# First attention pair rearranged, and one step of the feed-forward moved into the last pair

## The chip, the cores and the metric

The kernel runs on one NeuronCore of a Trainium2 chip. TensorE (PE) multiplies matrices; VectorE (DVE), ScalarE (ACT) and GpSimd (POOL) do the elementwise work; SyncE (SP) issues the loads. The engines run side by side and meet at semaphores; each takes its own instructions in order. The metric is the device time of one execution in microseconds (us), lower is better. Before the change it is 503.4 us, the median of three runs (503.26 to 503.74).

## What is computed

Attention over 2 batches x 12 heads, 448 tokens, head size 64, all fp32, then two feed-forward blocks on the 896 tokens:

```python
scores = cap * np.tanh(q @ k.T / np.sqrt(64) / cap)     # cap = 30
attn = np.exp(scores - max) / (sum + 1e-09);  x = attn @ v
h = x @ w_in                                            # 768 -> 1024
solu = h * softmax(h)
x = ((solu - mean) / sqrt(var + 1e-06) * g_ln) @ w_out  # 1024 -> 768
g = x @ w_gate;  val = x @ w_val                        # 768 -> 1536
out = silu(g) * val @ w_out2                            # 1536 -> 768
```

The weights come as float64 and are rounded to fp32 on the chip. Each product whose operands are split into a high and a low part (`hi`, `lo`) is three matmuls (hi*hi, hi*lo, lo*hi); the sums S, the products with v (pv) and the warm products are plain fp32 and are recorded as two instructions each.

## The kernel before

Attention goes over 12 pairs of heads (`attn_pair`, L276). A pair has these steps:

- `attn_load` (L180): q, k and v of the pair, each as two loads of 112 KB on SyncE's queue.
- `attn_T` (L192): TensorE transposes q and k into a PSUM tile T, four pieces each; then the high part is copied out of T by ScalarE (by VectorE for pair 1) and the low part is subtracted by VectorE. Both go to `ks`. For pair 0 that is done for k first and then for q, in one T tile of two banks; for the other pairs k and q go together.
- `attn_qk` (L208): chunk c of four: six matmuls `sc` over the two heads, into one of two score buffers, then one tanh on ScalarE (112 x 896).
- `attn_exp` (L223): one exp on ScalarE over two chunks.
- `attn_sums`, `attn_recip`, `attn_pv`, `attn_norm` (L229 to L274) of the pair before: column sums S by TensorE, their reciprocals by GpSimd and VectorE (the tiles tr and sm), the products pv, and x = pv * tr split into hi and lo.

Between them VectorE makes a twelfth of w_in per pair out of float64 (the tiles wi). While `in_order` is set (all of attention), each engine's instructions stay in the order of the code; after L553 a scheduler may move them. Pair 0 and pair 1 take chunks 2 and 3 late in the pair (`early` is false); from pair 2 on they come right after the first exp. A thirteenth call of `attn_pair` finishes pair 11, and three of the six steps of h_0 (the first 128 tokens of x @ w_in, six matmuls a step) fill in there; the other three follow (L550 to L552). Then h_1, h_2, ... come, each with a softmax tail on VectorE and ScalarE (`tail`, L368).

PSUM has eight banks. Up to L557 two pools hold them: `psc` two score buffers of two banks, and `ptA` one buffer for each tag, laid out in the order in which the tags are first used: pv (the warm products use it too), t (two banks: T, and h_0), S. Then the pool `pm` (L560) takes all eight as buffers of one bank each; a tile of `pm` can be written only when the last reader of what lay in its bank is done. The two tail reads of h_0 that come last are these, one for each half f of h:

```python
self.V.scalar_tensor_tensor(ef, ef, sm[:, 6:7], h[f], op0=ALU.mult, op1=ALU.mult,
```

`keep_warm(n)` (L174) issues n products of zeros that nothing reads.

Of the kernel before, what the change touches and what calls it, by code (L numbers as in the profile page):

```python
# [5 lines left out]
F32 = mybir.dt.float32  # L6
# [30 lines left out]
class Kernel:  # L37
# [154 lines left out]
    def attn_T(self, i):  # L192

        CP, S = self.CP, self.S
        r = self.raws[i]
        ks = r["ks"] = self.at.tile([128, 2, 2, S], F32R, name=f"ks_{i}", tag="ks", bufs=2)
        ps = self.pt.tile([128, 2, 512], F32, name=f"T_{i}", tag="t")
        lots = ("k", "q") if i == 0 else ("kq",)
        for names in lots:
            for n in names:  # L200
                m = "kq".index(n)
                for c in range(4):
                    self.transpose(ps[:, m, c * CP:(c + 1) * CP], r[n][:, c * 128:(c + 1) * 128], self.ident[:CP, :CP])
            m = slice("kq".index(names[0]), "kq".index(names[-1]) + 1)
            (self.hi_dve if i == 1 else self.hi_act)(ks[:, m, 0], ps[:, m, :S])
            self.lo_dve(ks[:, m, 1], ps[:, m, :S], ks[:, m, 0])

    def attn_qk(self, i, c):  # L208

# [66 lines left out]
    def attn_pair(self, i, fill=()):  # L276


        last, n = i - 1, 2 * self.NP
        if i == 0:  # L280
            self.attn_load(2, "v")
            self.w_in_load(1)
        elif i + 2 < n:
            self.attn_load(i + 2)
        w = self.w_steps[i]

        early = i > 1
        w[0]()
        if i < n:
            self.attn_qk(i, 0)  # L290
            self.attn_qk(i, 1)
        if i + 1 < n:
            self.attn_T(i + 1)
        if i < n:
            self.attn_exp(i, 0)
            if early:
                self.attn_qk(i, 2)
                self.attn_qk(i, 3)
        for f in fill:
            f()  # L300
        if i:
            self.attn_sums(last)
        w[1]()
        w[2]()
        if i:
            self.attn_pv(last, 0)
            self.attn_pv(last, 1)
            self.attn_recip(last)
        w[3]()
        if i < n:  # L310
            if not early:
                self.attn_qk(i, 2)
                self.attn_qk(i, 3)
            self.attn_exp(i, 1)
        if i:
            self.attn_pv(last, 2)
            self.attn_pv(last, 3)
            self.attn_norm(last)
# [198 lines left out]
    def run(self):  # L517
# [7 lines left out]
        self.at = self.pool("at", side="right")  # L525
        psc = self.psc = self.pool("psc", bufs=2, space=PSUM)
        ptA = self.pt = self.ph = self.pool("ptA", bufs=1, space=PSUM)
        self.attn_load(0, "kq")
        self.setup()
        self.attn_load(1, "kq")  # L530
        self.wi = [self.slot(f"wi{u}", [128, KD, F1], f"wi{u}") for u in range(2)]
# [3 lines left out]
        w = [self.w_in_steps(i) for i in range(2 * KD)]  # L535
        none = lambda: None
        w = [(none,) * 4] + w + [(none,) * 4]
        self.w_steps = [(w[i][1], w[i][2], w[i + 1][0], w[i][3]) for i in range(2 * KD + 1)]
        self.attn_T(0)
        self.keep_warm(4)  # L540
        self.attn_load(0, "v")
        self.attn_load(2, "kq")
        self.w_in_load(0)
        self.attn_load(1, "v")
        nc.sync.dma_start(self.gt, self.g_ln.rearrange("(f p) -> p f", p=128))
        h = [self.ff1_h(t) for t in range(7)]
        for i in range(2 * self.NP):
            self.attn_pair(i)
        self.htag = "t"
        self.attn_pair(2 * self.NP, [f for _, f in h[0][:3]])  # L550
        for _, f in h[0][3:]:
            f()  # L552
        self.in_order = False  # L553
        self.at.release()
# [110 lines left out]
```

## Time and profile before

| | |
|---|---|
| median of 3 runs | 503.4 us |
| the profiled execution | 504.33 us |
| its span, first to last instruction | 502.0 us |
| PE busy, DVE busy, ACT busy | 492.1 (98%), 351.9 (70%), 251.1 (50%) us |
| mean granted TensorE clock | 0.997 |
| attention, about | 0 to 118 us |
| h and its tails, about | 117 to 176 us |

The profile is one execution; times in it count from the first instruction. A row of the timeline gives start and length of a group of equal instructions, and in brackets how long the engine stood idle before it and which instruction's end released it. A granted clock of 1.00 is 2.4 GHz, 0.50 is 1.2 GHz.

### The profile page before, as it was taken

The numbers are of one execution on the slowest core, as the hardware profiler recorded it, in microseconds if no ns is written. First come the engines' busy times: TensorE is split into PE (matmuls) and PEld (weight loads), VectorE is DVE, ScalarE is ACT, GpSimd is POOL, SyncE is SP. The second block draws the span as 40 slices with busy tenths as digits, with TensorE's granted clock in tenths as the row PEclk, the third lists the DMA queues.
The fourth block names the chain that finished last, engine by engine and source line by source line (L and its number), as shares of the span: only waits on it lengthen the run. The fifth ranks groups of instructions, "written<-read, shape, count | busy, mean of one in ns | idle before, by whom it ended". The sixth has DMA issues, their size and how long they took to land.

```text
span 502.0 us, 7647 instructions
## 1 busy us (share of the span) xinstructions
PE 492.1 (98%) x3016; PEld 406.1 (81%) x3016; DVE 351.9 (70%) x633; ACT 251.1 (50%) x373; POOL 21.9 (4%) x62
## 2 busy tenths in 40 slices
PE   7899999999999999999999999999999999999996
PEld 6454545456788899898899998889999989999996
DVE  2689999984778894769899999788997867200000
ACT  4999999961224695666544454444434434100000
POOL 1112121210000010000000000000000000000000
PEclk9899999999999999999999999999999999999999
DMA  6856564311000222243535445446344525111111
GB/s 146 218 130 165 129 164 117 103 44 42 1 0 23 76 73 85 85 146 128 185 127 164 151 144 172 125 127 188 96 126 104 179 64 157 33 33 31 33 31 31
DMA packets 66916, 52.40 MB, mean 104 GB/s; under 512 B 35904, under 2 KB 62272, under 8 KB 66880
## 3 DMA queue, kind: packets, MB, share of 16 engines
q1 hardware_dynamic: 66112, 51.13, 35.3%
q10 hardware_dynamic: 736, 0.79, 0.4%
q8 instruction: 23, 0.38, 0.3%
q14 instruction: 13, 0.11, 0.1%
q0 software_dynamic: 32, 0.00, 0.0%
HBM read 49.16 MB, written 2.75 MB: 103 GB/s over the span
## 4 chain that ended last, share of the span: by engine, by line
PE 94%; ACT 3%; DVE 2%; issue 0%; POOL 0%; POOLq 0%
PE o L29 17%; PE g L29 17%; PE v L29 17%; PE x L29 11%; PE h L29 10%; PE pv L29 7%; PE sc L29 6%; PE S L29 4%; PE T L29 2%; ACT P L29 2%; PE lt L29 1%; DVE sm L29 1%; PE warm L29 1%; DVE e L29 0%; ACT e L29 0%
## 5 line engine op out<-in xcount | busy, mean ns | idle before, releaser
L29 PE MATMUL g<-x,y 128*128 128x512 f32 (+1 forms) x432 | 91.2, 363 | 0.0
L29 PE MATMUL v<-x,y 128*128 128x512 f32 (+1 forms) x432 | 90.5, 362 | 0.0
L29 PEld LDWEIGHTS g<-x,y 128*128 128x128 f32 x432 | 78.5, 188 | 8.9
L29 PEld LDWEIGHTS v<-x,y 128*128 128x128 f32 x432 | 78.2, 188 | 8.5
L29 PE MATMUL h<-wi,x 128*128 128x512 f32 x252 | 58.9, 392 | 0.0
L29 PEld LDWEIGHTS h<-wi,x 128*128 128x128 f32 x252 | 46.9, 188 | 11.0 <-issue 1.5
L29 PE MATMUL o<-x,a 128*128 128x384 f32 x294 | 52.3, 334 | 0.0
L29 PEld LDWEIGHTS o<-x,a 128*128 128x128 f32 x294 | 51.1, 188 | 0.0
L29 ACT ACTIVATE P<-sc,consts 112x896 f32<-112x896 f32 x48 | 45.8, 1009 | 5.7 <-PE sc L29 5.7
L29 ACT ACTIVATE P<-P,consts 112x1792 f32<-112x1792 f32 x24 | 43.0, 1794 | 0.5
L29 PE MATMUL sc<-ks 64*112 64x448 f32 x288 | 37.0, 385 | 2.7 <-ACT P L29 2.4
L504 ACT ACTIVATE ob<-o 128x384 f32<-128x384 f32 x14 | 6.9, 492 | 64.0 <-PE o L29 64.0
L29 PE MATMUL pv<-P,v 112*32 112x448 f32 x384 | 38.5, 539 | 0.0
L29 PE MATMUL x<-lB,wo 128*128 128x256 f32 (+1 forms) x192 | 37.3, 338 | 0.4 <-ACT lB L29 0.4
L29 PEld LDWEIGHTS sc<-ks 64*112 64x112 f32 x288 | 23.3, 174 | 17.3 <-issue 6.6
L29 PE MATMUL o<-y,a 128*128 128x384 f32 x189 | 34.1, 334 | 0.0
L29 PEld LDWEIGHTS x<-lB,wo 128*128 128x128 f32 x192 | 30.1, 189 | 3.6 <-ACT lB L29 0.6
L29 PEld LDWEIGHTS o<-y,a 128*128 128x128 f32 x189 | 32.9, 188 | 0.1
L29 PEld LDWEIGHTS pv<-P,v 112*32 112x32 f32 x384 | 12.3, 110 | 23.5 <-issue 23.2
L29 PE MATMUL x<-lA,wo 128*128 128x384 f32 x144 | 28.5, 336 | 0.0
L29 PEld LDWEIGHTS x<-lA,wo 128*128 128x128 f32 x144 | 25.1, 188 | 1.1
L29 DVE SCALAR_TENSOR_TENSOR w<-w_raw,w 128x768 uint32<-128x768 uint32 (+1 forms) x26 | 23.1, 891 | 0.3
(90 smaller groups left out, 628.1 us busy)
## 6 DMA issues: line engine op xcount, KB each, us to landing
wg_raw<-in_moe_w_gate_dram SPq DMA_DIRECT2D x12, 768.0 KB, 4.2
wv_raw<-in_moe_w_val_dram SPq DMA_DIRECT2D x12, 768.0 KB, 4.2
w_raw<-in_moe_w_out_dram SPq DMA_DIRECT2D x11, 768.0 KB, 4.5
wi_raw<-in_moe_w_in_dram SPq DMA_DIRECT2D x12, 512.0 KB, 4.7
wo_raw<-in_moe_w_out_dram SPq DMA_DIRECT2D x12, 512.0 KB, 3.4
k<-in_k_dram SPq DMA_DIRECT2D x24, 112.0 KB, 2.9
q<-in_q_dram SPq DMA_DIRECT2D x24, 112.0 KB, 4.0
v<-in_v_dram SPq DMA_DIRECT2D x24, 112.0 KB, 2.9
```

The costliest lines, as they stand in the source:

```text
L29: i = f(*a, **k)
L504: nc.scalar.activation(ob, acc, AF.Copy)
```

## The change

Pair 0: q is loaded and transposed ahead of k, into a tile of its own (with the tag S, one bank), and k into a one-bank tile of tag t. k's high and low parts are made for the first chunk (112 columns) and then for the other 336. The four chunks of pair 0 are issued in a row, then pair 1's transposes, then 14 warm products. Two warm products stand after q's transposes; the four after both are gone. Pair 1 takes chunks 2 and 3 early. The first step of h_0 moves from the thirteenth call into pair 11, between its chunks 1 and 2; the other five come after pair 11's pv.

```diff
--- before.py
+++ after.py
@@ -194,16 +194,23 @@
         CP, S = self.CP, self.S
         r = self.raws[i]
         ks = r["ks"] = self.at.tile([128, 2, 2, S], F32R, name=f"ks_{i}", tag="ks", bufs=2)
-        ps = self.pt.tile([128, 2, 512], F32, name=f"T_{i}", tag="t")
-        lots = ("k", "q") if i == 0 else ("kq",)
-        for names in lots:
-            for n in names:
-                m = "kq".index(n)
+        if i:
+            ps = self.pt.tile([128, 2, 512], F32, name=f"T_{i}", tag="t")
+            lots = [(ps, "kq", S)]
+        else:
+            ps = [self.pt.tile([128, 512], F32, name=f"T_{n}", tag=t) for n, t in (("q", "S"), ("k", "t"))]
+            lots = [(p.unsqueeze(1), n, w) for p, n, w in zip(ps, "qk", (S, CP))]
+        for ps, names, w in lots:
+            for j, n in enumerate(names):
                 for c in range(4):
-                    self.transpose(ps[:, m, c * CP:(c + 1) * CP], r[n][:, c * 128:(c + 1) * 128], self.ident[:CP, :CP])
+                    self.transpose(ps[:, j, c * CP:(c + 1) * CP], r[n][:, c * 128:(c + 1) * 128], self.ident[:CP, :CP])
             m = slice("kq".index(names[0]), "kq".index(names[-1]) + 1)
-            (self.hi_dve if i == 1 else self.hi_act)(ks[:, m, 0], ps[:, m, :S])
-            self.lo_dve(ks[:, m, 1], ps[:, m, :S], ks[:, m, 0])
+            for a in (slice(0, w), slice(w, S)):
+                if a.start < a.stop:
+                    (self.hi_dve if i == 1 else self.hi_act)(ks[:, m, 0, a], ps[:, :, a])
+                    self.lo_dve(ks[:, m, 1, a], ps[:, :, a], ks[:, m, 0, a])
+            if names == "q":
+                self.keep_warm(2)
 
     def attn_qk(self, i, c):
 
@@ -284,20 +291,24 @@
             self.attn_load(i + 2)
         w = self.w_steps[i]
 
-        early = i > 1
         w[0]()
         if i < n:
             self.attn_qk(i, 0)
             self.attn_qk(i, 1)
+        if i == 0:
+            self.attn_qk(i, 2)
+            self.attn_qk(i, 3)
         if i + 1 < n:
             self.attn_T(i + 1)
+        if i == 0:
+            self.keep_warm(14)
+        for f in fill:
+            f()
         if i < n:
             self.attn_exp(i, 0)
-            if early:
-                self.attn_qk(i, 2)
-                self.attn_qk(i, 3)
-        for f in fill:
-            f()
+        if 0 < i < n:
+            self.attn_qk(i, 2)
+            self.attn_qk(i, 3)
         if i:
             self.attn_sums(last)
         w[1]()
@@ -308,9 +319,6 @@
             self.attn_recip(last)
         w[3]()
         if i < n:
-            if not early:
-                self.attn_qk(i, 2)
-                self.attn_qk(i, 3)
             self.attn_exp(i, 1)
         if i:
             self.attn_pv(last, 2)
@@ -525,7 +533,7 @@
         self.at = self.pool("at", side="right")
         psc = self.psc = self.pool("psc", bufs=2, space=PSUM)
         ptA = self.pt = self.ph = self.pool("ptA", bufs=1, space=PSUM)
-        self.attn_load(0, "kq")
+        self.attn_load(0, "qk")
         self.setup()
         self.attn_load(1, "kq")
         self.wi = [self.slot(f"wi{u}", [128, KD, F1], f"wi{u}") for u in range(2)]
@@ -537,18 +545,17 @@
         w = [(none,) * 4] + w + [(none,) * 4]
         self.w_steps = [(w[i][1], w[i][2], w[i + 1][0], w[i][3]) for i in range(2 * KD + 1)]
         self.attn_T(0)
-        self.keep_warm(4)
         self.attn_load(0, "v")
         self.attn_load(2, "kq")
         self.w_in_load(0)
         self.attn_load(1, "v")
         nc.sync.dma_start(self.gt, self.g_ln.rearrange("(f p) -> p f", p=128))
         h = [self.ff1_h(t) for t in range(7)]
+        self.htag = "t"
         for i in range(2 * self.NP):
-            self.attn_pair(i)
-        self.htag = "t"
-        self.attn_pair(2 * self.NP, [f for _, f in h[0][:3]])
-        for _, f in h[0][3:]:
+            self.attn_pair(i, [f for _, f in h[0][:1]] if i == 2 * self.NP - 1 else ())
+        self.attn_pair(2 * self.NP)
+        for _, f in h[0][1:]:
             f()
         self.in_order = False
         self.at.release()
```

TensorE's order at the start, before the change (T is the tile of the transposes, sc_0 to sc_3 the chunks; numbers behind names are buffers):

```order
L29 MATMUL warm<-z 64x64 x18
L29 MATMUL T_129<-ident,k_73 128x112 x4
L29 MATMUL T_129<-ident,q_76 128x112 x4
L29 MATMUL warm<-z 64x64 x4
L29 MATMUL sc_0_168<-ks_128 112x448 x6
L29 MATMUL sc_1_176<-ks_128 112x448 x6
L29 MATMUL T_185<-ident,k_119 128x112 x4
L29 MATMUL T_185<-ident,q_122 128x112 x4
L29 MATMUL sc_2_204<-ks_128 112x448 x6
L29 MATMUL sc_3_212<-ks_128 112x448 x6
L29 MATMUL sc_0_233<-ks_184 112x448 x6
L29 MATMUL sc_1_241<-ks_184 112x448 x6
```

The same stretch after it:

```order
L29 MATMUL warm<-z 64x64 x18
L29 MATMUL T_q<-ident,q_73 128x112 x4
L29 MATMUL warm<-z 64x64 x2
L29 MATMUL T_k<-ident,k_76 128x112 x4
L29 MATMUL sc_0_169<-ks_128 112x448 x6
L29 MATMUL sc_1_177<-ks_128 112x448 x6
L29 MATMUL sc_2_186<-ks_128 112x448 x6
L29 MATMUL sc_3_194<-ks_128 112x448 x6
L29 MATMUL T_203<-ident,k_119 128x112 x4
L29 MATMUL T_203<-ident,q_122 128x112 x4
L29 MATMUL warm<-z 64x64 x14
L29 MATMUL sc_0_249<-ks_202 112x448 x6
```

Pair 1's transposes moved behind all four chunks of pair 0, and 14 products stand between them and pair 1's first chunk.

TensorE's order at the end of attention, where h_0's last step meets h_1 (h_1_0 and h_1_1 are the two halves of h_1; in brackets which engine's semaphore the instruction waits for), before:

```order
L29 MATMUL h_0_1366<-wi0_125,x_127 128x512 [waits DVE_49]
L29 MATMUL h_0_1366<-wi1_126,x_127 128x512
L29 MATMUL h_0_1366<-wi1_126,x_127 128x512 [waits DVE_49]
L29 MATMUL h_0_1366<-wi0_125,x_127 128x512 x2
L29 MATMUL h_1_0_1479<-wi0_125,x_127 128x512
L29 MATMUL h_1_1_1480<-wi0_125,x_127 128x512 [waits PE_49]
```

and after the change:

```order
L29 MATMUL h_0_1315<-wi0_125,x_127 128x512 [waits DVE_49]
L29 MATMUL h_0_1315<-wi1_126,x_127 128x512
L29 MATMUL h_0_1315<-wi1_126,x_127 128x512 [waits DVE_49]
L29 MATMUL h_0_1315<-wi0_125,x_127 128x512 x2
L29 MATMUL h_1_0_1495<-wi0_125,x_127 128x512
L29 MATMUL h_1_1_1496<-wi0_125,x_127 128x512 [waits DVE_49]
```

The order is the same; h_1_1's first matmul waited for TensorE's own S of pair 11 and now waits for VectorE. In the built program T and h_0 lay in banks 5 and 6 and S in bank 7; now S has bank 5, and T and h_0 have 6 and 7, since pair 0's q takes the tag S ahead of the tag t. h_1_1 lies in bank 7 in both. The VectorE instruction that it waits for now is the read of h_0's second half named above.

TensorE around the last pair (pair 11's chunks, then sums and pv of pairs 10 and 11), before:

```order
L29 MATMUL sc_0_1283<-ks_1203 112x448 x6
L29 MATMUL sc_1_1291<-ks_1203 112x448 x6
L29 MATMUL sc_2_1301<-ks_1203 112x448 x6
L29 MATMUL sc_3_1309<-ks_1203 112x448 x6
L29 MATMUL S_1317<-P_0_1186,ones 32x448 x4
```

and after:

```order
L29 MATMUL sc_0_1299<-ks_1219 112x448 x6
L29 MATMUL sc_1_1307<-ks_1219 112x448 x6
L29 MATMUL h_1315<-wi_125,x 128x512 x2
L29 MATMUL h_1315<-wi_126,x 128x512 x2
L29 MATMUL h_1315<-wi_125,x 128x512 x2
L29 MATMUL sc_2_1324<-ks_1219 112x448 x6
```

Six of h_0's 36 matmuls came forward; the twelve that followed them between pv of pair 10 and S of pair 11 went behind pv of pair 11.

## Rows read from the trace of the kernel before

**Rows 1.** Chain that ended last, shares of the span by engine.

```profile
PE 94%; ACT 3%; DVE 2%; issue 0%; POOL 0%; POOLq 0%
```

**Rows 2.** Second load of q: its issue (start, length), then size and landing.

```profile
2.84 0.62 SPq L190 DMA_DIRECT2D q<-in_q_dram  x1
...
q<-in_q_dram SPq DMA_DIRECT2D x1, 112.0 KB, 3.3
```

**Rows 3.** Timeline of PE, first pairs: start, length, what, idle before it and releaser.

```profile
4.90 0.57 PE L29 MATMUL T<-ident,k 112*128 112x112 f32 x4
6.76 0.60 PE L29 MATMUL T<-ident,q 112*128 112x112 f32 x4 [1.29 <-DVE ks L29]
7.30 0.68 PE L29 MATMUL warm<-z 128*64 128x64 f32 x8
...
14.04 2.36 PE L29 MATMUL sc<-ks 64*112 64x448 f32 x12 [1.79 <-ACT P L29]
...
24.23 1.47 PE L29 MATMUL sc<-ks 64*112 64x448 f32 x12
...
33.12 1.48 PE L29 MATMUL sc<-ks 64*112 64x448 f32 x12
...
36.84 1.71 PE L29 MATMUL S<-P,ones 112*32 112x448 f32 x16
...
41.49 1.47 PE L29 MATMUL sc<-ks 64*112 64x448 f32 x12
```

**Rows 4.** Timeline of ACT, first two pairs, and the last exp of attention.

```profile
7.40 0.54 ACT L29 ACTIVATE ks<-T 128x448 fp32r<-128x448 f32 x1 [1.35 <-PE T L29]
9.36 1.91 ACT L29 ACTIVATE P<-sc,consts 112x896 f32<-112x896 f32 x2 [1.41 <-PE sc L29]
...
16.62 1.89 ACT L29 ACTIVATE P<-sc,consts 112x896 f32<-112x896 f32 x2
18.40 0.92 ACT L29 ACTIVATE ks<-T 128x896 fp32r<-128x896 f32 x1
...
22.10 1.91 ACT L29 ACTIVATE P<-sc,consts 112x896 f32<-112x896 f32 x2 [1.11 <-PE sc L29]
...
106.57 1.79 ACT L29 ACTIVATE P<-P,consts 112x1792 f32<-112x1792 f32 x1
```

**Rows 5.** Windows: busy us (count) of PE, PEld, DVE, ACT, POOL; clock, DMA share, GB/s.

```profile
14.50:15.00 0.50, 0.49 (x6) 0.07 (x4) 0.05 (x1) 0.47 (x2) 0.00 (x0) 0.74 0.96 110
15.00:15.50 0.50, 0.50 (x4) 0.43 (x6) 0.47 (x2) 0.50 (x1) 0.00 (x0) 0.50 0.55 38
...
18.00:18.50 0.50, 0.50 (x9) 0.23 (x12) 0.00 (x0) 0.50 (x2) 0.00 (x0) 0.84 0.82 279
```

**Rows 6.** Timeline of PE, end of attention and first rows of h.

```profile
100.11 1.48 PE L29 MATMUL sc<-ks 64*112 64x448 f32 x12
102.08 1.75 PE L29 MATMUL sc<-ks 64*112 64x448 f32 x12 [0.49 <-ACT P L29]
...
117.37 12.58 PE L29 MATMUL h<-wi,x 128*128 128x512 f32 x54
130.47 1.09 PE L29 MATMUL lt<-ident,e 128*128 128x128 f32 x8 [0.53 <-DVE e L29]
```

**Rows 7.** Timeline of DVE: pair 0's low part, pair 1's high part.

```profile
7.98 0.62 DVE L29 TENSOR_TENSOR ks<-T,ks 128x448 fp32r<-128x448 f32 x1 [1.27 <-ACT ks L29]
10.88 1.09 DVE L29 CAST ks<-T 128x896 fp32r<-128x896 f32 x1 [2.27 <-PE T L29]
```

**Rows 8.** Timeline of DVE: normalization of pair 10, then the tail of h_0.

```profile
105.53 0.65 DVE L29 STREAM_TRANSPOSE tr<-S 128x448 f32<-128x448 f32 x1 [1.24 <-PE S L29]
...
109.54 0.61 DVE L29 TENSOR_TENSOR x<-pv,tr 128x448 f32<-128x448 f32 x1
...
121.82 1.29 DVE L29 TENSOR_REDUCE sm<-h 128x1 f32<-128x512 f32 x2 [2.17 <-PE h L29]
...
126.72 0.73 DVE L29 SCALAR_TENSOR_TENSOR e<-e,sm,h 128x512 f32<-128x512 f32 x1
```

## The prediction

> **What bounds the kernel now.** I read the chain that ended last first: TensorE holds 94% of it, ScalarE 3% [rows 1]. So what counts is where TensorE stands still, and the timelines of TensorE and of the engines that it waits for come next. Two places matter. At the start TensorE waits for the first pair's softmax: its second transposes wait 1.29 us, and before 14.04 it is idle for 1.79 us [rows 3], while ScalarE from 9.36 to 16.62 has no gap [rows 4]. From 33.12 on a pair takes 41.49 - 33.12 = 8.37 us without a stall [rows 3]. At the end of attention it waits 0.49 us once more, and from 117.37 on 54 matmuls of h run as one stream up to the first transposes of h_0's result, which wait 0.53 us for VectorE [rows 6]. A third thing is the clock: 0.74 in the half microsecond from 14.50, 0.50 from 15.00, and 0.84 in that from 18.00 [rows 5]. By these shares it is at 1.2 GHz from about 14.74 to 18.16, right after the idle 1.79 us; 3.4 us at half rate lose 1.7 us of matmul time.
>
> **First pair.** The second load of what comes second lands at 2.84 + 3.3 = 6.1 [rows 2]; that is k now, of the same size. T_k no longer shares a tile with what is read, so its transposes run from 6.15 to 6.75 instead of from 6.76 [rows 3]; q's two parts are made in the meantime. ScalarE's copy of 448 columns takes 0.54, of 896 0.92 [rows 4], so 0.38 per 448 and 0.26 for 112; VectorE's 0.62 and 1.09 [rows 7] give 0.27. So the first chunk's high part is there at 7.05, its low part at 7.4. Twelve score matmuls, two chunks, take 1.48 us [rows 3]; one chunk issues in half of that, 0.7, and with the run-out of its last matmul, which the half doesn't shorten, I take 0.95: begun at 7.1 it ends at 8.05, and tanh starts there instead of at 9.36: 1.3 earlier. The other 336 columns: ScalarE's 0.45 wait until VectorE has read the first part, then VectorE takes 0.51, so that chunk 1 is done at 8.9, under the first tanh, which ends at 9.05: nothing.
>
> ScalarE then does the same four tanh and two exp in another order, 7.26 us as before (9.36 to 16.62, [rows 4]), plus 0.06 since chunk 2 has to wait for a score buffer: pair 1's tanh starts at 15.4, not 16.62. Behind it pair 1's chunk 3 starts when the second tanh ends, at 15.4 + 1.9 = 17.3, lasts 0.7, and S and pv (41.49 - 36.84 = 4.65, [rows 3]) bring pair 2's first chunk to 22.7; before it was at 24.23. Pair 2 then took 33.12 - 24.23 = 8.89, since ScalarE came late after its 1.11 us wait [rows 4]; that wait goes, so pair 2 takes 8.37. Pair 3 starts at 31.05 instead of 33.12: **-2.05 us**.
>
> What I cost at nothing: pair 1's transposes move behind four chunks and end at 10.05 + 0.7 + 1.0 = 11.75 (chunk 3 starts when the second tanh ends); VectorE's two copies of 1.09 [rows 7] end at 14.0, pair 1's first chunk at 14.7, under ScalarE's 15.4. The 14 warm products are 28 instructions; eight took 0.68 [rows 3], so 28 take some 1.8 and end at 13.5, before the copies. If that cover went (the products at half rate, 3.0 us), it would cost 0.15. The two products after T_q end before k has landed. SyncE's queue only swaps two loads, and a load of w_in passes half a load of k that is used a pair later. In the new order no idle stretch of TensorE is longer than 0.6 us, so I let the clock stay up. Bounds: -2.5 (if ScalarE never waits and the period is even shorter at first) and -0.4 (if the clock falls all the same and 1.7 come back).
>
> **Last pair.** Six matmuls of h_0 come between chunks 1 and 2. In the stream of 54 one takes 12.58 / 54 = 0.23 [rows 6]. The six, 1.5 us with the change of shape, fill the 0.49 and the 0.27 by which the second twelve (1.75) are longer than the first (1.48) [rows 6]: -0.75. The price: pv of pair 11 now comes right behind S of pair 11, and its bank is free only when VectorE has read pair 10's pv. That read ends 110.15 - 105.53 = 4.62 after VectorE's first transpose [rows 8]. Counted from 100.11, S of pair 10 starts after 1.4 + 1.5 + 1.4 at 104.4, so this transpose comes at 104.4 + 1.71 = 106.1 and the read ends at 110.75; TensorE is there after S, pv (4.65) and S again (1.5), at 110.55, and waits 0.2. The last exp ends at 106.57 + 1.79 = 108.36 [rows 4], before S of pair 11 at 109.05. Together **-0.5**, between 0 and -0.75.
>
> **The bank of h_1.** This part the diff does not name. h_1's second half lies in bank 7, which was S's and is now h_0's second half. TensorE takes its instructions in order, so it stops at the first matmul of that half until VectorE's second read of e<-e,sm,h ends, at 126.72 + 0.73 = 127.45 in the old times [rows 8]. Before, that matmul was number 20 of the stream of 54: 117.37 + 19 x 0.233 = 121.8 [rows 6]. The wait is 127.5 - 121.8 = 5.7 us. The tail itself doesn't move against h_0's end: VectorE was idle for 2.17 us before it [rows 8] and has nothing more to do now. The 35 matmuls left take 35 x 0.233 = 8.15, so the transposes of h_0 come at 135.65 instead of 130.47: the 0.53 us wait there is swallowed. **+5.2**, and I know no cover: nothing but h_1 is in the queue.
>
> A pause of 5.6 us is three times the 1.79 after which the clock fell [rows 5]. I take one stretch at half rate like that one, from the restart on: **+1.7**; bounds 0 (it is up again when work resumes) and 3.4 (twice as long).
>
> On the banks the Trainium skill has a rule (Perfetto Trace Analysis, section Matmuls): matmul groups that don't depend on each other should rotate through different PSUM banks, so that the evacuation of one overlaps the next group's matmuls. The trace agrees for the old layout: the stream of 54 ran straight on while VectorE read h_0 [rows 6, 8]. By that rule the overlap of 5.7 us is lost for as long as one bank is shared, and the sum is the one above.
>
> Behind that all is TensorE's stream again: h_1's tail starts when h_1 ends, as before.
>
> **Sum.** -2.05 - 0.5 + 5.2 + 1.7 = +4.35, against the profiled execution's 504.33 (span 502.0, 2.3 around it): 508.7 there. That execution is 0.9 above the median of 503.4, so I set the change on the median: 507.7.
>
> **Rivals.**
> 1. The clock does not cost: it is up when work resumes. For it: in the first pair it fell only 0.7 us after the matmuls had begun again. Against it: the pause is three times as long. Sum +2.65, 506.0. The skill (TensorE: Matmul & The Clock Gate, section Why this matters for your kernels) says that an idle gap between bursts takes the engine back to half rate, which speaks against this rival; no run here shows a gap of this length.
> 2. The clock stays low twice as long: +6.05, 509.4.
> 3. The first pair gains next to nothing, as k lands late or the clock falls there still: -0.4 in place of -2.05, +6.0, 509.4. Against it: landing is read from a row, and ScalarE's chain starts 1.3 earlier by terms of which none is above 0.6.
> 4. The other side: h_1_1 doesn't hold TensorE up, because other matmuls pass the one that waits. Then -2.05 - 0.5 remain: 500.8, faster. It decides as soon as the engine can find 5.6 us of work behind it; the 35 matmuls of h_1 include 17 that write the other half. Against it: while the transposes of h_0 waited 0.53 us, no matmul of h_2 ran, though nothing held these back but their place [rows 6]. If half of the wait went so, the sum would be about nothing: 503.4.
>
> **Chances.** Forecast (507.7, with 506.8 to 508.7) 0.64; rival 1 0.13; rival 2 0.08; rival 3 0.06; rival 4 0.06 with all its gain and 0.03 with half. Below 505.3 lie rival 4's 0.09; above 509.2 about half of rivals 2 and 3, 0.07: the range is 505.3 to 509.2. About 0.2%, 1 us, is what a measurement can tell from no change. Faster 0.06, same 0.03, slower 0.91.
>
> **What would show it.** The first tanh at about 8.05, pair 3's first chunk at 31, no clock below 1.00 before 100; h's six matmuls between the last pair's chunks with no wait there; then an idle time of about 5.6 us on TensorE at h, released by VectorE's e, and a clock of 0.50 around the restart; the transposes of h_0 without a wait. I am wrong if the stream of h has no such gap, if the clock is 1.00 right behind it, or if pair 3 starts after 32.

## The result and the profile after

The changed kernel takes 508.02 us, the median of five runs (507.82 to 508.87), against 503.4 before: 1.0092 of it, with a 95% interval of 1.0079 to 1.0106. It is slower by 4.6 us, where 507.7 was forecast.

The profiled execution has a span of 506.2 us, 4.2 more than before. The rows below come from it, in the order of the prediction. First TensorE's timeline from the start to pair 3 (start and length in us, what, idle before it and who ended that), against [rows 3]:

```profile
5.02 0.98 PE L29 MATMUL T_q<-ident,q 112*128 112x112 f32 x4
...
6.31 0.60 PE L29 MATMUL T_k<-ident,k 112*128 112x112 f32 x4
7.27 1.79 PE L29 MATMUL sc<-ks 64*112 64x448 f32 x12 [0.35 <-ACT ks L29]
...
11.88 1.84 PE L29 MATMUL warm<-z 128*64 128x64 f32 x28
...
22.73 1.48 PE L29 MATMUL sc<-ks 64*112 64x448 f32 x12
...
31.12 1.48 PE L29 MATMUL sc<-ks 64*112 64x448 f32 x12
```

The waits of 1.29 and 1.79 us are gone; the longest left in this stretch is 0.35. Pair 2 begins at 22.73 instead of 24.23, pair 3 at 31.12 instead of 33.12. ScalarE, against [rows 4]:

```profile
6.95 0.26 ACT L29 ACTIVATE ks<-T_k 128x112 fp32r<-128x112 f32 x1 [0.37 <-PE T_k L29]
...
8.18 3.90 ACT L29 ACTIVATE P<-sc,consts 112x896 f32<-112x896 f32 x4 [0.17 <-PE sc L29]
...
15.34 1.89 ACT L29 ACTIVATE P<-sc,consts 112x896 f32<-112x896 f32 x2
...
23.64 1.01 ACT L29 ACTIVATE P<-sc,consts 112x896 f32<-112x896 f32 x1 [0.31 <-PE sc L29]
```

The four tanh of pair 0 stand in one row from 8.18 on (9.36 before), and the wait of 1.11 us ahead of pair 2's tanh is 0.31. So the first pair does what the change says. TensorE from pair 11 on, against [rows 6]:

```profile
98.16 1.47 PE L29 MATMUL sc<-ks 64*112 64x448 f32 x12
99.56 1.66 PE L29 MATMUL h<-wi,x 128*128 128x512 f32 x6
101.15 1.49 PE L29 MATMUL sc<-ks 64*112 64x448 f32 x12
...
107.10 1.69 PE L29 MATMUL S<-P,ones 112*32 112x448 f32 x16
109.06 3.21 PE L29 MATMUL pv<-P,v 112*32 112x448 f32 x32 [0.27 <-DVE x L29]
112.20 7.36 PE L29 MATMUL h<-wi,x 128*128 128x512 f32 x31
125.05 9.93 PE L29 MATMUL h<-wi,x 128*128 128x512 f32 x35 [5.49 <-DVE e L29]
134.82 1.04 PE L29 MATMUL lt<-ident,e 128*128 128x128 f32 x8
```

Here most of the loss sits in a single row. Before, 54 matmuls of h ran as one stream; now the stream breaks after 31, TensorE stands 5.49 us, and `<-DVE e` names VectorE's read of h_0. Pair 11 was 1.95 us early at 98.16, and h_0's transposes (lt) are 4.35 us late at 134.82. VectorE's tail of h_0, against [rows 8], shows which read ends the wait:

```profile
124.27 0.73 DVE L29 SCALAR_TENSOR_TENSOR e<-e,sm,h 128x512 f32<-128x512 f32 x1
...
127.16 0.81 DVE L29 TENSOR_SCALAR e<-e,sm 128x1024 f32<-128x1024 f32 x1
```

The second `e<-e,sm,h` ends at 125.00, and TensorE goes on at 125.05. The tail of h_0 ends at 127.97 while TensorE is still busy, so lt, which waited 0.53 us for it before, waits no more. The clock around the pause, in windows of half a microsecond (columns as in [rows 5], the clock third from the end):

```profile
121.50:122.00 0.50, 0.00 (x0) 0.00 (x0) 0.00 (x0) 0.50 (x3) 0.00 (x0) 0.89 0.00 0
122.00:122.50 0.50, 0.00 (x0) 0.00 (x0) 0.07 (x1) 0.40 (x2) 0.00 (x0) 0.50 0.00 0
...
128.50:129.00 0.50, 0.50 (x3) 0.36 (x3) 0.00 (x0) 0.00 (x0) 0.00 (x0) 0.78 0.00 0
129.00:129.50 0.50, 0.50 (x4) 0.41 (x3) 0.00 (x0) 0.00 (x0) 0.00 (x0) 1.00 0.00 0
```

The granted clock goes to 1.2 GHz during the pause and stays there until about 128.7, some 3.7 us behind the restart. Over the first 100 us the column reads 1.00, through the stretch too in which it was 0.50 before. (In the first 6 us it disagrees with the durations: q's four transposes at 5.02 took 0.98 us and k's four at 6.31 took 0.60, both at a granted clock of 1.00.)

### The profile page after: what moved, and what is told of

Read it like the earlier page. It is cut to its first block, busy times and chain, and to the rows that moved or that the text cites. A ratio compares the mean times of both kernels' runs of the same rounds, so it can differ in the third digit from the quotient of the medians.

```text
span 506.2 us, 7696 instructions
## 1 busy us (share of the span) xinstructions
PE 494.4 (98%) x3040; PEld 408.6 (81%) x3040; DVE 352.1 (70%) x634; ACT 250.9 (50%) x374; POOL 21.3 (4%) x62
## 4 chain that ended last, share of the span: by engine, by line
PE 96%; DVE 2%; ACT 1%; issue 0%; POOL 0%; POOLq 0%
PE o L29 17%; PE g L29 17%; PE v L29 17%; PE h L29 12%; PE x L29 11%; PE pv L29 7%; PE sc L29 6%; PE S L29 4%; PE T L29 2%; PE lt L29 1%; PE warm L29 1%; DVE sm L29 1%; DVE ks L29 0%; ACT P L29 0%; ACT e L29 0%
## 5 line engine op out<-in xcount | busy, mean ns | idle before, releaser
L29 PE MATMUL h<-wi,x 128*128 128x512 f32 x252 | 60.8, 400 | 5.5 <-DVE e L29 5.5
L29 PEld LDWEIGHTS h<-wi,x 128*128 128x128 f32 x252 | 48.0, 193 | 16.9 <-DVE e L29 5.9
```

What stands on the lines that cost most here:

```text
L29: i = f(*a, **k)
```

## The experiments

The theory is the prediction's: the bank of h_1 costs about 5 us of waiting and 1.7 us of clock, and the two parts that the change is about gain some 2.5. The rival is that the loss comes from the new order of the instructions itself. All times are medians, and each ratio is against the kernel before, run on the same chip. The runs on h's step alone, on k in one piece, on the products left out and on before's places for the chunks shared a second chip, on which before takes 503.63 us against 503.43 on the first, so between the two groups 0.2 us of difference means nothing.

**The banks put back.** In the changed kernel k's tile is allocated ahead of q's. That changes no instruction and no place in any engine's row, but T and h_0 lie in banks 5 and 6 again and S in 7.

```
-            ps = [self.pt.tile([128, 512], F32, name=f"T_{n}", tag=t) for n, t in (("q", "S"), ("k", "t"))]
-            lots = [(p.unsqueeze(1), n, w) for p, n, w in zip(ps, "qk", (S, CP))]
+            pk, pq = [self.pt.tile([128, 512], F32, name=f"T_{n}", tag=t) for n, t in (("k", "t"), ("q", "S"))]
+            lots = [(p.unsqueeze(1), n, w) for p, n, w in zip((pq, pk), "qk", (S, CP))]
```

> The changed kernel with T_k's tile taken ahead of T_q's, so that T and h_0 lie in banks 5 and 6 and S in 7 again; every engine's order is that of the changed kernel. Bank theory: the pause in h (5.49 us) and the half-rate stretch behind it go, the first pair's 2.0 us and the last pair's 0.6 us stay: 500.8 us (500.3 to 501.3), the stream of h through the tail of h_0 has no gap, and the transposes of h_0 wait about 0.5 us for VectorE again. Rival (the move of h_0's steps does it: all of h_0 now stands right ahead of h_1, with nothing between): as slow as the changed kernel, 508.

Measured: 501.32 us, ratio 0.9959 (0.9947 to 0.9972). TensorE's timeline at the end of attention in this kernel:

```profile
98.20 1.47 PE L29 MATMUL sc<-ks 64*112 64x448 f32 x12
...
109.09 3.21 PE L29 MATMUL pv<-P,v 112*32 112x448 f32 x32 [0.26 <-DVE x L29]
112.24 15.26 PE L29 MATMUL h<-wi,x 128*128 128x512 f32 x66
128.02 1.09 PE L29 MATMUL lt<-ident,e 128*128 128x128 f32 x8 [0.53 <-DVE e L29]
```

The 66 matmuls run as one stream, and lt waits 0.53 us as it did before the change. h's stream begins within 0.04 us of the changed kernel's, and lt then comes 6.80 us earlier. So the layout of the banks alone costs 508.02 - 501.32 = 6.7 us, and the rest of the change gains: the rival is out.

**The banks alone, in the kernel before.** One of its 18 first warm products gets a tile of tag S ahead of T; nothing else is touched.

```
-        self.keep_warm(18)
+        self.keep_warm(17)
+        self.keep_warm(1, "S")
...
-    def keep_warm(self, n):
-        ps = self.pt.tile([128, 512], F32, name="warm", tag="pv")
+    def keep_warm(self, n, tag="pv"):
+        ps = self.pt.tile([128, 512], F32, name="warm", tag=tag)
```

> The kernel before with one of its 18 first warm products put into a tile of the tag S, ahead of T: S gets bank 5 there, T and h_0 get 6 and 7; every engine's order is that of before. Bank theory: the wait alone, 5.7 us less the 0.53 us swallowed at the transposes, and 1.6 us of half rate behind it: 510.2 us (509.3 to 510.9). Rival (the move of h_0's steps does it): 503.4.

Measured: 510.39 us, ratio 1.0140 (1.0126 to 1.0154), so 7.0 us more. The same row appears on TensorE:

```profile
116.89 4.64 PE L29 MATMUL h<-wi,x 128*128 128x512 f32 x19
127.02 10.10 PE L29 MATMUL h<-wi,x 128*128 128x512 f32 x35 [5.49 <-DVE e L29]
```

The stream breaks after 19 matmuls, the number that the prediction counted in the old order, for the same 5.49 us. Counted from pair 11's first chunk (99.58) to lt (136.95), so without what the first pair did in this execution, it is 37.37 us against 130.47 - 100.11 = 30.36 before [rows 6]: 7.0 again. The price goes with the banks in either order of instructions.

**The pause filled.** In the changed kernel 44 products of zeros stand between h_0 and h_1; the wait stays.

```
+        self.keep_warm(44)
```

> The changed kernel with 44 warm products (88 instructions, 0.058 us each, 5.1 us) between h_0's last step and h_1. If the clock is a term of its own: it stays at 1.00, the 35 matmuls of h_1 behind the wait take 8.1 us instead of 9.93, and the time falls by 1.7 to 506.3 (505.9 to 506.8) though the wait stays where it is. Rival (the pause is all the cost, the clock costs nothing): 508.0, or a little more if the products end late.

Measured: 506.54 us, ratio 1.0058 (1.0046 to 1.0071).

```profile
112.54 7.10 PE L29 MATMUL h<-wi,x 128*128 128x512 f32 x30
119.57 5.35 PE L29 MATMUL warm<-z 128*64 128x64 f32 x88
124.84 8.72 PE L29 MATMUL h<-wi,x 128*128 128x512 f32 x36
133.40 1.04 PE L29 MATMUL lt<-ident,e 128*128 128x128 f32 x8
```

The clock is 1.00 behind the products, too:

```profile
125.00:125.50 0.50, 0.49 (x2) 0.18 (x3) 0.47 (x2) 0.00 (x0) 0.00 (x0) 1.00 0.00 0
```

From the start of h's stream to lt it takes 133.40 - 112.54 = 20.86 us; in the changed kernel it was 134.82 - 112.20 = 22.62, with the banks put back 128.02 - 112.24 = 15.78. The products end at 119.57 + 5.35 = 124.92, and VectorE's read that frees the bank at 125.30 in this execution, so they don't lengthen the wait. By the traces, then, the wait costs 20.86 - 15.78 = 5.1 us and the low clock 22.62 - 20.86 = 1.8; by the medians the clock costs 508.02 - 506.54 = 1.5. Part of that difference arises ahead of h: pair 11 began 0.35 us later in the profiled execution of this kernel (98.51 against 98.16).

**The move of h's step alone.** In the kernel before, the first step of h_0 goes between chunks 1 and 2 of pair 11 and the rest behind pv(11). Its first pair and its banks stay.

```
-            if early:
-                self.attn_qk(i, 2)
-                self.attn_qk(i, 3)
         for f in fill:
             f()
+        if i < n and early:
+            self.attn_qk(i, 2)
+            self.attn_qk(i, 3)
...
+        self.htag = "t"
         for i in range(2 * self.NP):
-            self.attn_pair(i)
-        self.htag = "t"
-        self.attn_pair(2 * self.NP, [f for _, f in h[0][:3]])
-        for _, f in h[0][3:]:
+            self.attn_pair(i, [f for _, f in h[0][:1]] if i == 2 * self.NP - 1 else ())
+        self.attn_pair(2 * self.NP)
+        for _, f in h[0][1:]:
```

> The kernel before with h_0's first step moved into pair 11 as in the change, and the other five behind pv of pair 11; nothing else, banks as before. By the sum: the 0.49 and 0.27 us at pair 11's chunks go, 0.27 come at pv of pair 11: 502.9 (502.6 to 503.2). Rival (h_0's steps one after the other cost more than that): 503.4 or above.

Measured: 503.04 us over eleven runs, ratio 0.9986 (0.9975 to 0.9998); before on the same chip 503.63, so 0.6 us less. The interval reaches from 0.1 to 1.3 us, so the size rests on TensorE's rows:

```profile
99.71 1.48 PE L29 MATMUL sc<-ks 64*112 64x448 f32 x12
101.12 1.66 PE L29 MATMUL h<-wi,x 128*128 128x512 f32 x6
...
110.59 3.21 PE L29 MATMUL pv<-P,v 112*32 112x448 f32 x32 [0.24 <-DVE x L29]
...
129.51 1.09 PE L29 MATMUL lt<-ident,e 128*128 128x128 f32 x8 [0.53 <-DVE e L29]
```

From pair 11's first chunk to lt it takes 29.80 us, against 130.47 - 100.11 = 30.36 before [rows 6]: 0.56 less, with the new wait at pv that the prediction named.

**k in one piece.** With the banks put back, k's parts are made for all 448 columns at once.

```
-            lots = [(p.unsqueeze(1), n, w) for p, n, w in zip((pq, pk), "qk", (S, CP))]
+            lots = [(p.unsqueeze(1), n, w) for p, n, w in zip((pq, pk), "qk", (S, S))]
```

> As e1_banks_back, but k's high and low parts are made for all 448 columns at once. If the split in 112 and 336 columns counts: the first chunk's low part is ready some 0.5 us later (0.54 and 0.62 us instead of 0.26 and 0.27), the first tanh starts at 8.75 instead of 8.18, and as ScalarE is the chain from there to pair 2, the time is 0.5 above e1_banks_back, 501.8. Rival (one extra wait in the split eats it: the 336 columns wait for VectorE): the same as e1_banks_back, 501.3.

Measured: 501.63 us, ratio 0.9964 (0.9951 to 0.9976); 0.3 above the version with k split, of which 0.2 can be the chip. The timeline of ScalarE shows the first tanh at 8.63, behind a longer wait:

```profile
8.63 3.88 ACT L29 ACTIVATE P<-sc,consts 112x896 f32<-112x896 f32 x4 [1.22 <-PE sc L29]
```

With k split it starts at 8.21 in the kernel with the banks put back, and pair 3 at 31.16 instead of 31.53. But k's load landed later there: its transposes began at 6.38, and here at 6.26. Counted from them, the first tanh comes 2.37 us later without the split and 1.83 with it, and pair 3 is 0.49 later. By the traces, one execution each, the split of k is worth about 0.5 us of the first pair's gain, as expected; the medians alone don't show it.

**The warm products left out.** With the banks put back, the 14 products ahead of pair 1's first chunk go.

```
-        if i == 0:
-            self.keep_warm(14)
```

> As e1_banks_back without the 14 warm products behind pair 1's transposes. TensorE then stands still for about 1.9 of the 2.3 us from 11.95 to 14.25. If the products hold the clock: it falls to 0.50 for some 3.4 us, pair 1's transposes for pair 2 and its chunks run at half rate, 0.5 to 1.5 us lost, 502.2. Rival (ScalarE is the chain there and hides it, or the clock holds): 501.3.

Measured: 501.47 us, ratio 0.9965 (0.9953 to 0.9977). The five executions lie apart: 502.31 and 502.29, with a mean clock of 0.996, and 501.21 to 501.47, with 0.998 to 1.000. The profiled one is of the first kind:

```profile
13.06 0.46 PE L29 MATMUL sc<-ks 64*112 64x448 f32 x2 [1.28 <-DVE ks L29]
14.10 1.61 PE L29 MATMUL sc<-ks 64*112 64x448 f32 x10 [0.57 <-DVE ks L29]
...
23.79 1.47 PE L29 MATMUL sc<-ks 64*112 64x448 f32 x12
```

Its clock in windows:

```profile
14.50:15.00 0.50, 0.50 (x8) 0.45 (x6) 0.00 (x0) 0.50 (x1) 0.00 (x0) 0.83 1.21 182
15.00:15.50 0.50, 0.50 (x4) 0.06 (x2) 0.00 (x0) 0.50 (x2) 0.00 (x0) 0.50 0.63 31
...
18.00:18.50 0.50, 0.50 (x8) 0.40 (x6) 0.47 (x2) 0.50 (x2) 0.00 (x0) 0.75 0.78 194
```

TensorE waits 1.28 and 0.57 us, the clock falls just behind, and pair 2 comes at 23.79 instead of 22.77. So both theories hold, each in some executions: without the products the clock falls in some of them and that costs 1.0 us, and in the others the products are worth nothing. The median hides this. Only the fall in the profiled execution is seen in a trace; the other four are told apart by their mean clock and time alone. The edit also lets two loads of w_in change places with half a load of k on SyncE's queue, but behind pair 0 TensorE waits for no load in this trace.

**Before's places for chunks 2 and 3.** With the banks put back, pairs 0 and 1 issue these chunks where the kernel before had them, and the 14 products go.

```
-        if i == 0:
-            self.attn_qk(i, 2)
-            self.attn_qk(i, 3)
...
-        if i == 0:
-            self.keep_warm(14)
...
-        if 0 < i < n:
+        if 1 < i < n:
...
+            if i < 2:
+                self.attn_qk(i, 2)
+                self.attn_qk(i, 3)
```

> As e1_banks_back, but pairs 0 and 1 take chunks 2 and 3 where the kernel before has them, and the 14 warm products are left out. If the new place of the chunks gives the second part of the 2.0 us: the first tanh is early as in e1_banks_back (8.18, against 9.36), but TensorE pauses again ahead of pair 1, the clock falls there, and pair 2 starts 1.2 and not 1.5 us early and has its 0.5 us stall: 502.1 (501.8 to 502.4). Rival (the gain is all from q and k at the start): 501.3.

Measured: 503.4 us over twelve runs, but from 501.58 to 505.73; ratio 0.9992 (0.9978 to 1.0006). Neither number was met. The profiled execution, one of 503.95 us, shows why the time doesn't answer the question. On TensorE, up to pair 3:

```profile
12.71 1.77 PE L29 MATMUL sc<-ks 64*112 64x448 f32 x12 [1.49 <-ACT P L29]
...
21.52 1.47 PE L29 MATMUL sc<-ks 64*112 64x448 f32 x12
...
25.76 1.01 PE L29 MATMUL T<-ident,q 112*128 112x112 f32 x4 [2.23 <-DMA q<-in_q_dram]
26.70 2.55 PE L29 MATMUL sc<-ks 64*112 64x448 f32 x12
```

and on SyncE's queue:

```profile
18.15 0.57 SPq L190 DMA_DIRECT2D q<-in_q_dram  x1
18.82 0.56 SPq L89 DMA_DIRECT2D wi_raw<-in_moe_w_in_dram  x1
19.43 0.56 SPq L190 DMA_DIRECT2D q<-in_q_dram  x1
```

In the kernel with the banks put back the two half loads of q stood together here, at 17.97; the edit has put a load of w_in between them. In this execution q's transposes waited 2.23 us for their load, and the next twelve score matmuls took 2.55 us, as the clock was 0.50 from 26.00 to 29.00. The fastest runs, 501.58 and 501.64, are 0.3 above the kernel with the banks put back, 0.2 of which can be the chip. That the load was in time in those is a guess, so what the row of four chunks is worth over the whole kernel stays open.

Ahead of that wait, though, the trace speaks against the theory. TensorE stood for 1.49 us ahead of pair 1, and the clock stayed at 1.00 up to 25.50. Pair 2's first chunk came at 21.52: not 1.2 but 2.7 us ahead of before's, and 1.25 ahead of the kernel with the banks put back (22.77), 0.21 of that since k's transposes began earlier (6.17 against 6.38). So in this execution the row of four chunks isn't what brings pair 2 forward.

**One step further.** With the banks put back, the second step of h_0 goes into the thirteenth call, ahead of S of pair 11, to cover the wait at pv.

```
-        self.attn_pair(2 * self.NP)
-        for _, f in h[0][1:]:
+        self.attn_pair(2 * self.NP, [f for _, f in h[0][1:2]])
+        for _, f in h[0][2:]:
```

> As e1_banks_back, with the second step of h_0 put ahead of S of pair 11, as cover for the 0.27 us by which pv of pair 11 waited for VectorE in the changed kernel. If that wait is a real term of the last pair: 0.25 below e1_banks_back, 500.55. If VectorE's work moves with it, the same time as e1_banks_back.

Measured: 501.01 us (500.93 to 501.32), ratio 0.9954 (0.9941 to 0.9968): 0.3 below the kernel with the banks put back, and the fastest version here, ahead of both kernels.

```profile
107.05 1.66 PE L29 MATMUL h<-wi,x 128*128 128x512 f32 x6
108.64 1.71 PE L29 MATMUL S<-P,ones 112*32 112x448 f32 x16
110.17 3.19 PE L29 MATMUL pv<-P,v 112*32 112x448 f32 x32
```

The wait of 0.26 us at pv is gone, but most of it is paid back: the six matmuls take 108.64 - 107.05 = 1.59 us here, and in the stream, at 0.231 each, 1.39. From pair 11's first chunk to lt it takes 127.73 - 98.00 = 29.73 us, against 128.02 - 98.20 = 29.82 with the banks put back: 0.1 less. The other 0.2 of the profiled execution's lead is there already at pair 11's first chunk; k's transposes began 0.23 us earlier in it (6.15 against 6.38). So the wait was a real term, but what covering it gains is nearer 0.1 than the 0.25 expected.

## Why the prediction was right

**First pair, -2.05.** Measured -2.00 at pair 3. The terms hold one by one: the first tanh at 8.18 (8.05 said), pair 1's at 15.34 (15.4), pair 2 at 22.73 (22.7). The 14 products took 1.84 us (1.8) and ended at 13.72, before they were needed. Costing them at nothing was right; what they buy shows where they were left out, as 1.0 us in two executions of five.

But -2.00 is the gain against one execution of before. Two more traces hold before's first pair unchanged. The move of h's step alone:

```profile
8.81 2.21 PE L29 MATMUL sc<-ks 64*112 64x448 f32 x10 [0.20 <-DVE ks L29]
...
32.70 1.47 PE L29 MATMUL sc<-ks 64*112 64x448 f32 x12
```

and the banks alone:

```profile
32.57 1.48 PE L29 MATMUL sc<-ks 64*112 64x448 f32 x12
```

In both the clock fell already in pair 0, behind the wait of 1.29 us (0.50 from about 8.5 and 8.1 on), and not again in pair 1. Pair 3 began at 32.70 and 32.57 instead of 33.12 [rows 3], so against them the gain is 1.6 and 1.45 us. The term fits the execution that it was read from, and is some 0.5 too large by these two and by the medians below.

**Last pair, -0.5.** Measured -0.56 alone, and the wait at pv is 0.27 (0.2 said).

**The bank of h_1, +5.2.** From the start of h's stream to the restart it takes 125.05 - 112.20 = 12.85 us, the 35 matmuls left add 35 x 0.231 = 8.1 (in the undisturbed stream one takes 15.26 / 66 = 0.231), and with the banks put back lt came after 15.78: 5.2 measured, 5.1 against the filled pause. The restart was placed right: with the banks alone, in the old order, it comes 127.02 - 116.89 = 10.13 us behind the start of the stream, and 127.5 - 117.37 = 10.13 was said. The pause reads 5.49 and not 5.7 since its start was counted at the spacing of the matmuls, and the last one runs on some 0.2 us longer (19 took 4.64, and 19 x 0.233 = 4.43 was said). The 35 matmuls left and the VectorE read that frees the bank were those named.

**The clock, +1.7.** From the restart to lt it takes 134.82 - 125.05 = 9.77 us, where 35 undisturbed matmuls take 8.1: a loss of 1.7 (1.8 by the filled pause, 1.5 by the medians). The stretch was longer than the one it was likened to, 6.8 us against 3.4, since it began in the pause; only the 3.7 us behind the restart cost anything. This was the least certain term: that a longer pause costs no more behind its end was assumed, and it held. The Trainium skill (TensorE: Matmul & The Clock Gate, section Why this matters for your kernels) says that a gap between bursts takes the engine back to half rate; the trace agrees, with 0.50 from 122.00 on.

**The sum, +4.35.** From the traces -2.00 - 0.56 + 5.2 + 1.7 = +4.3; lt itself is 4.35 late, and the span 4.2 longer. By the medians the two halves read a little otherwise. The kernel with the banks put back gains 503.43 - 501.32 = 2.1, not the 2.55 said, which fits a first pair worth 1.45 to 1.6 and not 2.05; the banks cost 6.7 (7.0 in the old order), where 6.9 was said. A gain 0.45 smaller and a price 0.2 smaller than said leave 4.6 against 4.35: the sum is off by less than one of its terms, and that much is luck; the mechanism is not.

**The rivals.** Rival 1 (the clock is free) and rival 2 (twice as long) fall with the clock back at 1.00 at 129.00 and the filled pause. Rival 3 falls with pair 3 at 31.12. Rival 4 (other matmuls pass the one that waits) falls with the two kernels in which only the banks differ: the 17 matmuls of h_1 for the other half did not run in the pause.

## What to carry to other kernels

Where one pool of PSUM tiles gives way to another, look up which old tile lies in the bank of each first new tile and when its last reader ends; a tag that is merely used earlier can move all of them. The diff doesn't show it where it costs, and in the order of TensorE's instructions only the engine that one of them waits for has changed. Read what an edit gains and what it breaks apart: here two parts worth 2.1 us came with a layout that cost 6.7, and two lines that swap an allocation keep the one without the other. When a median looks flat, look at the single executions beside their clock, as a fall in some of them alone is no small effect but a rare one. And read a gain from more than one trace of the kernel before where the clock can fall at one place or another: here it was 2.0 us against one and 1.5 against two others.

## What the runs showed of the hardware

- A short idle time early in the kernel does not take the clock down every time. In before's first pair the clock fell to 0.50 behind the wait of 1.29 us in two traces (h's step alone, the banks alone), where the later 1.06 and 1.18 us then left it at 1.00; in the third it stayed at 1.00 behind the 1.29 us and fell behind the later 1.79 [rows 3, 5]. With before's places for the chunks 1.49 us left it at 1.00. Without the warm products, waits of 1.28 and 0.57 us were followed by 0.50 in the profiled execution, and the mean clocks and times of the five set two of them apart by 1.0 us.
- The mean clock of an execution doesn't give its time. Of before's 23 executions on the second chip, the six with a mean clock of 0.999 to 1.000 have spans of 502.4 to 502.5 us, and the eight with 0.997 have 501.4 to 501.9. Why the former are longer no trace here shows.
- In a pause of 5.49 us the clock fell while TensorE was still idle, about 3 us before the restart, and came back 3.7 us behind it (some 3.9 with the banks alone); before, it fell after work had begun again and came back 3.4 us later. What the low clock cost in matmul time was near the same: 1.7 us measured behind the pause, and an estimate of 1.7 from the 3.4 us at half rate.
- One instruction that waits holds everything behind it on TensorE, also matmuls whose banks have long been free: in the pause of 5.49 us none of the 17 ran that write the other half of h_1, whose first matmul had run ahead of it.
